# Two edits to an attention and Fourier-mixing kernel: where the transposed outputs of attention are kept, and how the very last product leaves PSUM

## The chip, the cores and the metric

The kernel runs on one core of one Trainium2 chip. The metric is the device time of one execution in microseconds (us). Three executions of the kernel before took 1701.39, 1704.11 and 1705.67 us, so their median is 1704.11 us.

## The reference, cut to what matters

Two independent blocks over 2048 tokens of width 1024 are computed and stood side by side in the output's columns.

```python
# A: causal attention in a window of 256, 32 heads of 32
qkv = x @ wqkv                                   # 2048 x 1024 @ 1024 x 3072
scores = q @ k.T * 32 ** -0.5                    # kept where 0 <= query - key < 256
a = softmax(scores) @ v                          # then the heads side by side
a = a @ wo                                       # 1024 x 1024
# B: real part of a two-dimensional Fourier transform by matrices
y = dft_seq_re @ (x @ dft_hid_re.T) - dft_seq_im @ (x @ dft_hid_im.T)
out = concatenate([a, y], axis=-1)               # 2048 x 2048
```

All of it is in float32. The kernel holds each operand as a pair of float16 tiles, a high part and a low part, and multiplies three of the four pairings (`PASSES`, line 48).

## The kernel before, in words

**The stages.** First come the products for q, k and v (lines 939 to 975). Then the products of B run, in units that a list orders (lines 758 to 761, 1143 to 1191). Last comes the product with `wo` in eight turns of two row tiles each (lines 1196 to 1206). All the large products but the first ones go through `seven` (line 1037): seven products of half the size in place of eight, written to three PSUM banks called a, b and c in the order a, b, a, c, a, b, a. A bank is 512 float32 columns of 128 partitions. Every product is twelve matmuls of 512 columns, four blocks of depth by three passes.

**Attention is woven into this.** `attention` (line 211) is a generator, and `tick` (line 373) takes steps from it between the matmuls of the large products, so that TensorE alternates between them. It works in blocks of 128 queries of two heads. Four blocks make a chunk of 512 queries; there are 64 chunks, 8 groups of heads by 2 pairs of heads by 4 chunks of the sequence. `mm` and `vec` keep the written order on TensorE and, at first, on VectorE; the rest is ordered by the scheduler of the tile layer. It gives each tile of a pool a buffer, and makes the first writer of a new tile wait for the last user of the buffer.

**What a chunk goes through at its end.** `v_step` (line 295) multiplies the weights of two blocks with v into a PSUM bank `pv`, and VectorE sums its pieces into the chunk's tile `o` (line 323, the "reduce" below; two per chunk). After the second reduce `o_step` (line 327) normalises `o` in place (VectorE line 332, GpSimd line 334), makes the pair of high and low parts in a tile `ohl` (ScalarE line 337, GpSimd line 338), and issues a transposing DMA from `ohl` into a tile `ot` (line 340). Three blocks later another DMA stores `ot` to a scratch tensor `ots` in DRAM (line 360), from where the last stage loads it (line 1008). Both DMAs are issued by SP, as are the transposes of the weights of each block (line 277) and nearly all loads.

**The buffers of these three.** `o`, `ohl` and `ot` are taken from one ring of three buffers, `tag="o", bufs=3` (lines 301, 336 and 339). Which of the three buffers a tile gets is settled when the program is built, by which comes free first. In the built program 10 of the 64 first reduces wait for DMA queues and 54 for GpSimd; most of the transposes of line 340 wait for the store of the chunk before, which holds the buffer that they write.

**The last product.** In the last of the eight turns the product at position 6 goes on adding to bank a, as two halves of 256 columns (lines 1048 to 1066). After both halves VectorE evicts one (line 1062) and ScalarE the other (line 1064); each is then stored by a DMA of its own from SP. Nothing is left for TensorE then.

Of the kernel before, what the change touches and what calls it, by code (L numbers as in the profile page):

```python
# [9 lines left out]
F32 = mybir.dt.float32  # L10
F32R = mybir.dt.float32r
F16 = mybir.dt.float16
# [3 lines left out]
AF = mybir.ActivationFunctionType  # L16
ALU = mybir.AluOpType
AX = mybir.AxisListType

P = 128  # L20
# [3 lines left out]
DH = 32  # L24
# [29 lines left out]
def fused_kernel(ctx: ExitStack, tc: tile.TileContext, xa, wqk, wv, wo, xb, wd, cs, out):  # L54
# [58 lines left out]
    def mm(*args, **kwargs):  # L113
        with tc.issue_after(fixed[0].ins) if fixed else nullcontext():
            fixed[:] = [nc.tensor.matmul(*args, **kwargs)]  # L115
        return fixed[0]
# [94 lines left out]
    def attention():  # L211
# [83 lines left out]
        def v_step(b):  # L295

            g, hp, sc, i = blocks[b]
            pvb = ps_v.tile([P, CH], F32, tag="pv", name=f"pv_{b}")
            pvt = pvb[:, :4 * VW].rearrange("p (r h w) -> p r h w", r=2, h=2)
            if (g, hp, sc) not in cur:  # L300
                cur[g, hp, sc] = att.tile([P, QB, 2, DH + 1], F32, tag="o", bufs=3, name=f"o_{g}_{hp}_{sc}")
            for r in (1, 0):
                qb = sc * QB + i + r
                nb = min(qb + 1, 3)
                nt = min(nb, 2)
                d = st[b + r]

                def weights(part, j, kb):
                    if nb == 3 and kb == 0:
                        return d["z"][:, part * 2 + j]  # L310
                    return d["t"][:, (part * 2 + j) * nt + kb - (nb - nt)]

                seq = [(0, kb) for kb in range(nb)] + [(1, kb) for kb in range(nb)]
                for j in range(2):
                    at = j * VW
                    for m, (part, kb) in enumerate(seq):
                        w = VW if part == 0 else DH + 1
                        k = qb + 1 - nb + kb
                        mm(pvt[:, r, j, :w], weights(part, j, kb),
                           vts[g, hp, k // QB][:, k % QB, at:at + w],  # L320
                                         start=(m == 0), stop=(m == len(seq) - 1),
                                         skip_group_check=True)
            nc.vector.tensor_reduce(cur[g, hp, sc][:, i:i + 2], pvt.rearrange("p r h (k w) -> p r h w k", k=2),
                                    axis=AX.X, op=ALU.add)
            del st[b], st[b + 1]

        def o_step(g, hp, sc):

            o = cur.pop((g, hp, sc))
            rs = att.tile([P, 2 * QB], F32, tag="rs", name=f"rs_{g}_{hp}_{sc}")  # L330
            on = o.rearrange("p i h w -> p (i h) w")
            nc.vector.reciprocal(rs, on[:, :, DH])
            on = on[:, :, :DH]
            nc.gpsimd.tensor_tensor(on, on, rs.unsqueeze(2).to_broadcast([P, 2 * QB, DH]), op=ALU.mult)
            o = o[:, :, :, :DH]
            ohl = att.tile([P, QB, 2, DH, 2], F16, tag="o", bufs=3, name=f"ohl_{g}_{hp}_{sc}")
            nc.scalar.activation(ohl[:, :, :, :, 0], o, AF.Copy)
            nc.gpsimd.tensor_tensor(ohl[:, :, :, :, 1], o, ohl[:, :, :, :, 0], op=ALU.subtract)
            ot = att.tile([P, QB, P], F16, tag="o", bufs=3, name=f"ot_{g}_{hp}_{sc}")
            nc.sync.dma_start_transpose(ot, ohl.rearrange("p i h d a -> p (i h d a)"))  # L340
            store_o.append((ots[sc, g, hp].rearrange("c a t -> (c a) t"), ot.rearrange("p i q -> p (i q)")))

# [691 lines left out]
        part = lambda u, k: (lambda h, d: u[:, h, HG * k + d])  # L1034
        oq[q] = (whole(t1, 0), part(u1, 0), part(u2, 1), whole(t1, 1), part(u2, 0), whole(t2, 1), part(u1, 1))

    def seven(name, q, lhs, rhs, y1, y2, f, out_y, hook, where=None, parts=1):

        where = where or {r: (ps_m, perm[(k - turns[0]) % 3]) for k, r in enumerate("abc")}
        turns[0] += 1  # L1040

        banks = {r: pool.tile([P, CH], F32, tag=f"m{t}", name=f"{name}_{r}") for r, (pool, t) in where.items()}
        copy = lambda y, ps: behind_act.__setitem__(slice(None), [nc.scalar.activation(y, ps, AF.Copy, scale=f)])
        add = lambda y, ps: behind.__setitem__(
            slice(None), [nc.vector.scalar_tensor_tensor(y, ps, f, y, op0=ALU.mult, op1=ALU.add)])  # L1045
        for pos in range(7):
            ps = banks["abacaba"[pos]]
            if pos == 6 and parts > 1:
                out_y(2 * q, y1[:, :1], 0)
                w = CH // parts  # L1050
                for e in range(parts):
                    cols = slice(e * w, e * w + w)
                    m = 0
                    for k in range(4):
                        for hl, hr in PASSES:
                            mm(ps[:, cols], lhs[pos](hl, k), rhs(pos)[:, hr, k, cols], start=False,
                               stop=(m == 11), skip_group_check=True)
                            m += 1
                for e in range(parts):
                    cols = slice(e * w, e * w + w)  # L1060
                    if e % 2 == 0:
                        nc.vector.tensor_scalar(y1[:, 1, cols], ps[:, cols], f, None, op0=ALU.mult)
                    else:
                        nc.scalar.activation(y1[:, 1, cols], ps[:, cols], AF.Copy, scale=f)
                    out_y(2 * q, y1[:, 1:, cols], CH + e * w)
                return
            m = 0
            for k in range(4):
                for hl, hr in PASSES:
                    mm(ps, lhs[pos](hl, k), rhs(pos)[:, hr, k], start=(m == 0 and pos < 2),  # L1070
                                     stop=(m == 11), skip_group_check=True)
                    m += 1
                    if m % 4 == 0:
                        tick(4)
            if pos == 0:

                nc.scalar.activation(banks["c"], ps, AF.Copy)
            elif pos == 1:
                copy(y2[:, 1], ps)
            elif pos == 2:  # L1080
                copy(y2[:, 0], ps)
            elif pos == 3:
                copy(y1[:, 0], ps)
            elif pos == 4:
                add(y2[:, 1], ps)
            elif pos == 5:
                add(y2[:, 0], ps)
                out_y(2 * q + 1, y2)
            else:
                copy(y1[:, 1], ps)  # L1090
                out_y(2 * q, y1)
            hook(pos)
# [4 lines left out]
    with tc.tile_pool(name="pb", bufs=1) as pb:  # L1097
# [4 lines left out]
        def ytile():  # L1102
            ny[0] += 1
            return ybufs[ny[0] % 4]
# [91 lines left out]
        for q in range(NT // 2):  # L1196
# [6 lines left out]
                                                        y.rearrange("p e c -> p (e c)")),  # L1203
                  lambda turn: None,
                  {r: (ps_o, k) if q % 2 and k < 2 else (ps_m, perm[k]) for k, r in enumerate("abc")},
                  2 if q == NT // 2 - 1 else 1)


def _layout(inputs):
# [45 lines left out]
```

## Time and profile before

| | |
|---|---|
| median of three executions | 1704.11 us |
| the profiled execution's own time | 1701.5 us |
| its span, first to last instruction | 1699.8 us |
| TensorE busy | 1688.6 us, 99% of the span |
| VectorE, ScalarE, GpSimd busy | 1299.0, 1168.5, 575.2 us |
| granted TensorE clock over the span | 1.000 |
| chunks: reduces of line 323, transposes of line 340, stores of line 360 | 128, 64, 64 |

TensorE is busy nearly all the time, so time can be won or lost only where it waits, and before its first and after its last matmul. A row of the view of waits names the engine and the line that waited, what it waited for, the sum in us, how often, and the longest. A row of the timeline gives start, duration, engine, line, operation, tiles and shape, and in brackets the idle time of the engine before it with what ended it. PE is TensorE, DVE VectorE, ACT ScalarE, POOL GpSimd, SPq the queue of SP.

### The profile page before, as it was taken

Reading aid. Unit: us, or ns where it says so; the run is one execution under the profiler, and the core shown is the slowest. Engines: PE = TensorE matmul, PEld = TensorE weight load, DVE = VectorE, ACT = ScalarE, POOL = GpSimd, SP = SyncE. Lnnn points to the kernel's source line nnn. Section 1 sums busy time; section 2 is a strip of 40 time slices with the busy share of each in tenths; the row PEclk is TensorE's granted clock in tenths of the full one; section 3 lists DMA queues with packets and bytes.
Section 4 is the critical chain, followed back from the end, with each engine's and each line's share of the span. In section 5 each row is a group of like instructions: output and inputs, shape, how many; then the busy total and the mean of one; then the engine's idle time right before and its main releaser. Section 6 shows DMA issues by size and latency. Waiting matters only on the chain.

```text
span 1699.8 us, 30887 instructions
## 1 busy us (share of the span) xinstructions
PE 1688.6 (99%) x11007; PEld 847.7 (50%) x11007; DVE 1299.0 (76%) x2223; ACT 1168.5 (69%) x2035; POOL 575.2 (34%) x874
## 2 busy tenths in 40 slices
PE   9999999999999999999999999999999999999999
PEld 4444544555555555555554555545545545444444
DVE  7657787888987789897688896688876698687442
ACT  4476666676876787887787886688877688563322
POOL 0001222344434441444423565434555425411000
PEclk9999999999999999999999999999999999999999
DMA  6677999999999985987997999986989976866431
GB/s 244 240 267 245 252 289 269 282 264 306 256 240 209 211 220 127 206 194 184 232 251 236 199 186 176 227 197 127 190 161 204 226 183 137 177 180 121 115 99 75
DMA packets 469899, 348.63 MB, mean 205 GB/s; under 512 B 376944, under 2 KB 409968, under 8 KB 468848
## 3 DMA queue, kind: packets, MB, share of 16 engines
q1 hardware_dynamic: 462064, 321.48, 75.7%
q0 software_dynamic: 7680, 25.17, 9.5%
q8 instruction: 86, 1.41, 0.4%
q14 instruction: 69, 0.57, 0.1%
HBM read 166.99 MB, written 106.17 MB: 161 GB/s over the span
## 4 chain that ended last, share of the span: by engine, by line
PE 90%; DVE 3%; DMA 3%; ACT 2%; issue 1%; SPq 0%; POOL 0%; DVEq 0%; ACTq 0%; POOLq 0%
PE p_a L115 25%; PE pv L115 13%; PE p_b L115 12%; PE pq L115 10%; PE pk L115 10%; PE p_c L115 6%; PE po_a L115 5%; PE s L115 3%; PE po_b L115 2%; PE far L115 1%; PE po_c L115 1%; DMA ots<-ot 1%; DMA raw_wo<-in_wo_dram 1%; DVE reg L850 0%; DMA t<-hl 0%
## 5 line engine op out<-in xcount | busy, mean ns | idle before, releaser
L271 ACT ACTIVATE s<-s,bias,escs 128x256 f32<-128x256 f32 (+1 forms) x512 | 270.0, 528 | 11.7
L289 POOL TENSOR_SCALAR_AFFINE_SELECT z<-t 128x512 f16<-128x512 f16 x224 | 183.8, 828 | 162.2 <-PE pv L115 140.3
L264 ACT ACTIVATE bias<-mx,pshift,escs 128x2 f32<-128x2 f32 x256 | 98.4, 384 | 172.0 <-DVE mx L261 171.3
L275 DVE TENSOR_TENSOR hl<-s,hl 128x512 f16<-128x512 f32 (+1 forms) x256 | 170.2, 665 | 51.6 <-ACT hl L274 50.8
L115 PEld LDWEIGHTS <-reg 128*128 128x128 f16 x1344 | 128.9, 98 | 141.5
L291 POOL TENSOR_SCALAR_AFFINE_SELECT t<-t 128x512 f16<-128x512 f16 x224 | 187.8, 847 | 11.3
L115 PE MATMUL p_a<-reg,un_c 128*128 128x512 f16 x768 | 181.4, 379 | 0.6 <-DVE reg L850 0.3
L115 PE MATMUL pk<-reg,wu_k 128*128 128x512 f16 x768 | 174.2, 379 | 0.0
L268 POOL TENSOR_SCALAR mark<-bias 128x1 f32<-128x1 f32 x128 | 52.5, 410 | 358.3 <-ACT bias L264 333.6
L261 DVE TENSOR_REDUCE mx<-s 128x2 f32<-128x512 f32 (+1 forms) x256 | 170.9, 668 | 3.5
L115 PE MATMUL pv<-reg,reg 128*128 128x512 f16 x768 | 172.5, 379 | 0.0
L115 PEld LDWEIGHTS <-un_c 128*128 128x128 f16 x1152 | 109.9, 97 | 121.5 <-issue 2.2
L115 PEld LDWEIGHTS <-un_b 128*128 128x128 f16 x1152 | 109.6, 97 | 117.7 <-issue 0.9
L115 PEld LDWEIGHTS <-un_a 128*128 128x128 f16 x1152 | 109.4, 97 | 116.5
L115 PE MATMUL pq<-reg,wu_q 128*128 128x512 f16 x696 | 156.3, 379 | 0.0
L274 ACT ACTIVATE hl<-s 128x512 f16<-128x512 f32 (+1 forms) x256 | 148.8, 581 | 6.9 <-DMA t<-hl 1.4
L115 PE MATMUL p_a<-reg,un_b 128*128 128x512 f16 x576 | 136.4, 379 | 0.3 <-DVE y L1045 0.2
L115 PE MATMUL p_c<-reg,un_a 128*128 128x512 f16 x576 | 136.5, 379 | 0.0
L115 PE MATMUL p_b<-reg,un_b 128*128 128x512 f16 x576 | 136.3, 379 | 0.1
L115 PE MATMUL p_a<-reg,un_a 128*128 128x512 f16 x576 | 136.1, 379 | 0.0
L259 DVE COPY_PREDICATED s<-upper,far 128x256 f32<-128x256 uint32 x224 | 94.3, 421 | 46.3 <-PE s L115 45.3
L115 PEld LDWEIGHTS <-qk 96*128 96x128 f16 x1056 | 87.7, 97 | 66.4 <-issue 4.9
(216 smaller groups left out, 3139.7 us busy)
## 6 DMA issues: line engine op xcount, KB each, us to landing
raw_u<-in_cs_dram SPq DMA_DIRECT2D x64, 512.0 KB, 5.0
qk<-qk SPq DMA_DIRECT2D x64, 384.0 KB, 4.7
out_dram<-y POOLq DMA_DIRECT2D x72, 256.0 KB, 6.3
raw_wd<-in_wd_dram SPq DMA_DIRECT2D x24, 512.0 KB, 5.6
vs<-yv SPq DMA_DIRECT2D x32, 264.0 KB, 4.5
vt<-vs SPq DMA_DIRECT2D x64, 132.0 KB, 4.7
qk<-yq SPq DMA_DIRECT2D x32, 256.0 KB, 4.5
raw_wo<-in_wo_dram SPq DMA_DIRECT2D x16, 512.0 KB, 8.4
```

The lines of the kernel that those rows point to most:

```text
L115: fixed[:] = [nc.tensor.matmul(*args, **kwargs)]
L259: nc.vector.copy_predicated(s[:, :, P:], upper2, d["far"] if nb == 3 else never2)
L261: nc.vector.tensor_reduce(mx, sv, axis=AX.X, op=ALU.max, negate=True)
L264: nc.scalar.activation(bias, mx, AF.Identity, bias=pshift, scale=es)
L268: marks[:] = [nc.gpsimd.tensor_scalar(mark, bias[:, 0:1], 1.0, None, op0=ALU.mult)]
L271: nc.scalar.activation(sv[:, h], sv[:, h], AF.Exp, bias=bias[:, h:h + 1], scale=es)
L274: nc.scalar.activation(hi, sv, AF.Copy)
L275: behind[:] = [nc.vector.tensor_tensor(lo, sv, hi, op=ALU.subtract)]
L289: nc.gpsimd.affine_select(out=z, in_=pk, compare_op=ALU.is_gt, fill=0.0, base=0, pattern=[[0, 4], [-1, P]], channel_multiplier=1)
L291: nc.gpsimd.affine_select(out=pk, in_=pk, compare_op=ALU.is_ge, fill=0.0, base=0, pattern=[[0, 4], [1, P]], channel_multiplier=-1)
```

## The change

The first edit is in attention. `o` becomes a flat tile in a ring of two buffers, and `ohl` gets a tile of its own with one buffer. There is no tile for `ot` any more: the transposing DMA writes into the first bytes of the chunk's own `o`, read as float16, whose sums have been used up by then. The second edit is in the last turn of the last stage. Position 6 writes to two PSUM banks of its own, 384 columns and then 128 columns, and starts them fresh. What bank a held before (the sum of positions 0, 2 and 4) is evicted by ScalarE after position 4. VectorE then makes each of the two results as a scaled bank plus that evicted sum, into tiles of `ytile`, the 384 columns while the 128 are being multiplied. Each is stored from SP as before.

```diff
-                cur[g, hp, sc] = att.tile([P, QB, 2, DH + 1], F32, tag="o", bufs=3, name=f"o_{g}_{hp}_{sc}")
+                cur[g, hp, sc] = att.tile([P, QB * 2 * (DH + 1)], F32, tag="o", bufs=2, name=f"o_{g}_{hp}_{sc}")
...
-            ohl = att.tile([P, QB, 2, DH, 2], F16, tag="o", bufs=3, name=f"ohl_{g}_{hp}_{sc}")
+            ohl = att.tile([P, QB, 2, DH, 2], F16, tag="ohl", bufs=1, name=f"ohl_{g}_{hp}_{sc}")
...
-            ot = att.tile([P, QB, P], F16, tag="o", bufs=3, name=f"ot_{g}_{hp}_{sc}")
+            ot = held_o.bitcast(F16)[:, :QB * P].rearrange("p (i q) -> p i q", i=QB)
             nc.sync.dma_start_transpose(ot, ohl.rearrange("p i h d a -> p (i h d a)"))
...
+        ends = [(pool_, at_, w) for pool_, at_, w in (parts or ())]
+        halves = [pool_.tile([P, CH], F32, tag=f"m{t_}", name=f"{name}_e{k}") for k, ((pool_, t_), _, _) in enumerate(ends)]
+        lasts = [ytile()[:, 0, :w] for _, _, w in ends]
...
-                            mm(ps[:, cols], lhs[pos](hl, k), rhs(pos)[:, hr, k, cols], start=False,
+                            mm(e[:, :w], lhs[pos](hl, k), rhs(pos)[:, hr, k, cols], start=(m == 0),
...
-                    if e % 2 == 0:
-                        nc.vector.tensor_scalar(y1[:, 1, cols], ps[:, cols], f, None, op0=ALU.mult)
-                    else:
-                        nc.scalar.activation(y1[:, 1, cols], ps[:, cols], AF.Copy, scale=f)
-                    out_y(2 * q, y1[:, 1:, cols], CH + e * w)
-                return
+                    nc.vector.scalar_tensor_tensor(o, e[:, :w], f, y1[:, 1, cols], op0=ALU.mult, op1=ALU.add)
+                    out_y(2 * q, o.unsqueeze(1), CH + at_)
+                continue
...
             elif pos == 4:
                 add(y2[:, 1], ps)
+                if ends:
+                    copy(y1[:, 1], ps)
...
-                  2 if q == NT // 2 - 1 else 1)
+                  (((ps_o, 2), 0, 3 * P), ((ps_o, 3), 3 * P, P)) if q == NT // 2 - 1 else None)
```

Up to the last product the instructions of every engine stand in the same order as before; what changes there is what some of them wait for. On SP this is the piece around the transpose of chunk `6_0_2` (group 6, first pair, third chunk; 1211.2 us in the profiled execution) into `ot`, with the counters that each row waits for. The DMAs from SP use eight completion counters in turn, DMAHW0 to DMAHW7; each waits for the one that had its counter before, and the store two rows above the transpose uses DMAHW0.

```order
L277 DMA_TRANSPOSE t_207_15226<-hl_207_15223 128x8x128 [waits DMAHW7_49,DVE_49]
L360 DMA ots_59<-ot_6_0_1_15051 128x512 [waits DMAHW0_49]
L277 DMA_TRANSPOSE t_208_15273<-hl_208_15270 128x4x128 [waits DVE_49,DMAHW1_49,PE_49,Pool_49]
L340 DMA_TRANSPOSE ot_6_0_2_15315<-ohl_6_0_2_15312 128x4x128 [waits DMAHW2_49,DMAHW0_49,Pool_49]
L232 DMA vt_6_1_1_15506<-vs_58 128x4x132 [waits DMAHW3_49,PE_49]
L277 DMA_TRANSPOSE t_209_15353<-hl_209_15350 128x8x128 [waits DMAHW4_49,DVE_49]
```

The same piece of the changed kernel, whose line numbers are two higher:

```order
L277 DMA_TRANSPOSE t_207_15176<-hl_207_15173 128x8x128 [waits DMAHW7_49,DVE_49]
L362 DMA ots_59<-o_6_0_1_14849 128x512 [waits DMAHW0_49]
L277 DMA_TRANSPOSE t_208_15223<-hl_208_15220 128x4x128 [waits DVE_49,DMAHW1_49,PE_49,Pool_49]
L342 DMA_TRANSPOSE o_6_0_2_15111<-ohl_6_0_2_15262 128x4x128 [waits DMAHW2_49,Pool_49]
L232 DMA vt_6_1_1_15455<-vs_58 128x4x132 [waits DMAHW3_49,PE_49]
L277 DMA_TRANSPOSE t_209_15302<-hl_209_15299 128x8x128 [waits DMAHW4_49,DVE_49]
```

The transpose no longer waits for DMAHW0, the store of the chunk before; it still waits for GpSimd, which makes `ohl`, and for the eighth DMA before it.

On VectorE, at the first reduce of chunk `6_1_0`, two chunks later (the 105th of the 128 reduces, at 1237.38 us in the profiled execution), before:

```order
L259 COPY_PREDICATED s_214_15651<-upper_90,far_1040 128x2x128 [waits PE_49]
L261 TENSOR_REDUCE mx_214_15657<-s_214_15651 128x2 [waits DVE_49]
L122 SCALAR_TENSOR_TENSOR un33_a_15677<-raw_u33_0_15324,sc_u33_15635,un33_a_15677 128x1024 [waits DMAHW5_49,Activation_49]
L323 TENSOR_REDUCE o_6_1_0_15688<-pv_208_15687 128x132 [waits DMAHW3_49,DMAHW2_49,DMAHW6_49,DMAHW0_49,PE_49]
L807 TENSOR_TENSOR raw_u33_0_15324<-raw_u33_0_15324,raw_u33_1_15129 128x512 [waits DVE_49]
L275 TENSOR_TENSOR hl_213_15612<-s_213_15598,hl_213_15612 128x512 [waits DMAHW5_49,Activation_49]
```

And now:

```order
L259 COPY_PREDICATED s_214_15599<-upper_90,far_1040 128x2x128 [waits PE_49]
L261 TENSOR_REDUCE mx_214_15605<-s_214_15599 128x2 [waits DVE_49]
L122 SCALAR_TENSOR_TENSOR un33_a_15625<-raw_u33_0_15273,sc_u33_15583,un33_a_15625 128x1024 [waits DMAHW5_49,Activation_49]
L324 TENSOR_REDUCE o_6_1_0_15636<-pv_208_15635 128x132 [waits DMAHW2_49,DMAHW3_49,PE_49,Pool_49]
L809 TENSOR_TENSOR raw_u33_0_15273<-raw_u33_0_15273,raw_u33_1_15079 128x512 [waits DVE_49]
L275 TENSOR_TENSOR hl_213_15560<-s_213_15546,hl_213_15560 128x512 [waits DMAHW5_49,Activation_49]
```

DMAHW2 is the transpose of chunk `6_0_2` and DMAHW3 its store, so this reduce waits for the same store in both kernels. In the changed kernel 62 of the 64 first reduces wait for such a store, that of the chunk two before; in the kernel before 10 wait for DMA queues.

At the end of VectorE's program, before:

```order
L1045 SCALAR_TENSOR_TENSOR yo6_1_20171<-po6_a_20172,fo_110,yo6_1_20171 128x512 [waits DMAHW7_49,PE_49,Activation_49]
L1045 SCALAR_TENSOR_TENSOR yo6_1_20171<-po6_b_20173,fo_110,yo6_1_20171 128x512 [waits PE_49,Activation_49]
L1045 SCALAR_TENSOR_TENSOR yo7_1_20269<-po7_a_20270,fo_110,yo7_1_20269 128x512 [waits PE_49,Activation_49]
L1045 SCALAR_TENSOR_TENSOR yo7_1_20269<-po7_b_20271,fo_110,yo7_1_20269 128x512 [waits PE_49,Activation_49]
L1062 TENSOR_SCALAR yo7_0_20268<-po7_a_20270,fo_110 128x256 [waits PE_49]
```

And now:

```order
L1047 SCALAR_TENSOR_TENSOR yo6_1_20107<-po6_b_20109,fo_110,yo6_1_20107 128x512 [waits PE_49,Activation_49]
L1047 SCALAR_TENSOR_TENSOR yo7_1_20205<-po7_a_20206,fo_110,yo7_1_20205 128x512 [waits PE_49,Activation_49]
L1047 SCALAR_TENSOR_TENSOR yo7_1_20205<-po7_b_20207,fo_110,yo7_1_20205 128x512 [waits PE_49,Activation_49]
L1063 SCALAR_TENSOR_TENSOR y1_6757<-po7_e0_20209,fo_110,yo7_0_20204 128x384 [waits DMASW2_49,DMASW3_49,PE_49,Activation_49]
L1063 SCALAR_TENSOR_TENSOR y2_6758<-po7_e1_20210,fo_110,yo7_0_20204 128x128 [waits DMASW1_49,DMASW0_49,PE_49]
```

The eviction of line 1062 is replaced by two additions, of 384 and of 128 columns, and ScalarE's last instruction is no longer the second half but the 512 columns of bank a after position 4.

More of the change, by code (lines that the diff above doesn't have):

```diff
@@ L322, in v_step @@
                                          skip_group_check=True)
-            nc.vector.tensor_reduce(cur[g, hp, sc][:, i:i + 2], pvt.rearrange("p r h (k w) -> p r h w k", k=2),
+            o = cur[g, hp, sc].rearrange("p (i h w) -> p i h w", i=QB, h=2)
+            nc.vector.tensor_reduce(o[:, i:i + 2], pvt.rearrange("p r h (k w) -> p r h w k", k=2),
                                     axis=AX.X, op=ALU.add)
@@ L327, in o_step @@
         def o_step(g, hp, sc):
-            o = cur.pop((g, hp, sc))
+            held_o = cur.pop((g, hp, sc))
+            o = held_o.rearrange("p (i h w) -> p i h w", i=QB, h=2)
             rs = att.tile([P, 2 * QB], F32, tag="rs", name=f"rs_{g}_{hp}_{sc}")
@@ L1035, in o_blocks, with seven @@
         oq[q] = (whole(t1, 0), part(u1, 0), part(u2, 1), whole(t1, 1), part(u2, 0), whole(t2, 1), part(u1, 1))
-    def seven(name, q, lhs, rhs, y1, y2, f, out_y, hook, where=None, parts=1):
+    def seven(name, q, lhs, rhs, y1, y2, f, out_y, hook, where=None, parts=None):
         where = where or {r: (ps_m, perm[(k - turns[0]) % 3]) for k, r in enumerate("abc")}
@@ L1045, in seven @@
             slice(None), [nc.vector.scalar_tensor_tensor(y, ps, f, y, op0=ALU.mult, op1=ALU.add)])
+        ends = [(pool_, at_, w) for pool_, at_, w in (parts or ())]
+        halves = [pool_.tile([P, CH], F32, tag=f"m{t_}", name=f"{name}_e{k}") for k, ((pool_, t_), _, _) in enumerate(ends)]
+        lasts = [ytile()[:, 0, :w] for _, _, w in ends]
         for pos in range(7):
             ps = banks["abacaba"[pos]]
-            if pos == 6 and parts > 1:
+            if ends and pos == 6:
                 out_y(2 * q, y1[:, :1], 0)
-                w = CH // parts
-                for e in range(parts):
-                    cols = slice(e * w, e * w + w)
+                for e, o, (_, at_, w) in zip(halves, lasts, ends):
+                    cols = slice(at_, at_ + w)
                     m = 0
@@ L1055, in seven @@
                         for hl, hr in PASSES:
-                            mm(ps[:, cols], lhs[pos](hl, k), rhs(pos)[:, hr, k, cols], start=False,
+                            mm(e[:, :w], lhs[pos](hl, k), rhs(pos)[:, hr, k, cols], start=(m == 0),
                                stop=(m == 11), skip_group_check=True)
                             m += 1
-                for e in range(parts):
-                    cols = slice(e * w, e * w + w)
-                    if e % 2 == 0:
-                        nc.vector.tensor_scalar(y1[:, 1, cols], ps[:, cols], f, None, op0=ALU.mult)
-                    else:
-                        nc.scalar.activation(y1[:, 1, cols], ps[:, cols], AF.Copy, scale=f)
-                    out_y(2 * q, y1[:, 1:, cols], CH + e * w)
-                return
+                    nc.vector.scalar_tensor_tensor(o, e[:, :w], f, y1[:, 1, cols], op0=ALU.mult, op1=ALU.add)
+                    out_y(2 * q, o.unsqueeze(1), CH + at_)
+                continue
             m = 0
```

## The prediction

> **What bounds the kernel now.** I began with the page's busy times and then asked for the waits of TensorE alone (engine, tile and line, what was waited for, us in total, how often, the longest).
>
> ```profile
> PE 1688.6 (99%) x11007; PEld 847.7 (50%) x11007; DVE 1299.0 (76%) x2223; ACT 1168.5 (69%) x2035; POOL 575.2 (34%) x874
> ```
>
> ```profile
> PE far L115 <- DVE s L259: 4.3, 2, 3.2
> PE wps L735 <- DVE reg L727: 1.2, 1, 1.2
> PE p_a L115 <- DVE y L1045: 0.5, 2, 0.3
> PE pq L115 <- DMA wx<-in_xa_dram: 0.3, 1, 0.3
> PE p_a L115 <- DVE reg L850: 0.3, 1, 0.3
> PE p_a L115 <- ACT p_c L1077: 0.2, 1, 0.2
> ```
>
> TensorE bounds it. Of the span of 1699.8 us all but 11.2 are TensorE's own work, which the change leaves as it is except for the last product. The waits add up to 6.8 us, 1.2 of them before the first matmul. Most of what is left lies after the last one. So two places matter: the one long wait, 3.2 us, and the end. The end, in the timeline:
>
> ```profile
> 1687.89 2.75 PE L115 MATMUL po_a<-wx,uo 128*128 128x512 f16 x12
> 1688.09 0.69 ACT L1043 ACTIVATE yo<-po_c,fo 128x512 f32<-128x512 f32 x1 [1.90 <-PE po_c L115]
> 1688.80 8.44 SPq L1202 DMA_DIRECT2D out_dram<-yo  x4
> ...
> 1690.48 2.75 PE L115 MATMUL po_b<-wx,raw_o 128*128 128x512 f16 x12
> 1690.75 0.75 DVE L1045 SCALAR_TENSOR_TENSOR yo<-po_a,fo,yo 128x512 f32<-128x512 f32 x1 [14.79 <-PE po_a L115]
> ...
> 1693.07 2.78 PE L115 MATMUL po_a<-wx,uo 128*128 128x256 f16 x24
> ...
> 1695.89 0.48 DVE L1062 TENSOR_SCALAR yo<-po_a,fo 128x256 f32<-128x256 f32 x1 [1.80 <-PE po_a L115]
> 1696.41 0.47 ACT L1064 ACTIVATE yo<-po_a,fo 128x256 f32<-128x256 f32 x1 [7.63 <-DVE yo L1062]
> ```
>
> The last matmul ends at 1695.85, and then the two evictions run one after the other: both read bank a, and ScalarE's idle time is ended by VectorE's eviction. They end at 1696.88, the issue of the last store at 1697.24, and the span at 1699.8.
>
> **The last product, the certain part.** It removes 24 matmuls of 256 columns and adds twelve of 384 and twelve of 128. From start to start, twelve matmuls of 512 columns take 2.59 us (1687.89 to 1690.48), 216 ns each; 24 of 256 take about 2.62, 109 each. That is 0.42 ns a column and 2 ns besides, so one of 384 columns takes 162 ns, twelve 1.95. Matmuls of 128 columns stand elsewhere in the trace:
>
> ```profile
> 1240.01 0.22 PE L115 MATMUL far<-qk,qk 96*128 96x128 f16 x1 [3.21 <-DVE s L259]
> 1240.06 0.22 PE L115 MATMUL s<-qk,qk 96*128 96x128 f16 x1
> 1240.12 0.22 PE L115 MATMUL s<-qk 96*128 96x128 f16 x1
> ```
>
> They start 50 to 60 ns apart; with 55, twelve take 0.66, and the two parts 2.61: TensorE ends where it ended, within 0.05 us.
>
> The Trainium skill ("TensorE: Matmul & The Clock Gate", section "Back-to-back issue gap") speaks against narrow matmuls: it gives about 81 ns as the sustained spacing of pairs of weight load and matmul at 128 columns. By it the twelve would take 0.97 us, and the gain below would be about 0.34 instead of 0.65. The rows above, each with a weight load of its own, show 55, so I take 55.
>
> What follows the matmuls: VectorE's addition over 512 columns takes 0.75 us and its eviction of 256 took 0.48, about 1.05 ns a column and 0.21 fixed, so 0.62 for 384 and 0.35 for 128 (estimates from these two rows; the 128 lies in any case between 0.2 and 0.48). The 384 columns are complete at about 1693.07 + 1.95 + 0.16 = 1695.18, where the 0.16 is what a matmul lasts beyond its spacing (the last of 256 runs to 1695.85, 0.27 after its start). Their addition runs from 1695.22 to 1695.84, beside the narrow matmuls. The 128 columns are complete at 1695.84, and their addition runs from 1695.88 to 1696.23, where ScalarE ended at 1696.88 before. That is 0.65 earlier. SP ended the issue of the last store 0.36 us after its eviction; by that it is done with the first of the two at 1696.20, just as the second is wanted, and a loss of 0.05 is possible there. The store behind it and the end cost what they cost before. Bounds: from the two ends for the narrow addition, 0.5 to 0.8 us gained. Hidden is the new eviction of bank a after position 4. It is ScalarE's (0.69 by the row at 1688.09), it can start after VectorE's 0.75 at 1690.75, that is by 1691.5, and ends by 1692.2, 3 us before its first use. ScalarE has nothing else to do there (7.63 us idle), and no later matmul writes to bank a.
>
> **The buffers of attention.** No instruction is added or moved here; waits change. Removed is the wait of SP's transposes for the store of the chunk before. What SP waited for, and two neighbours from the list of all waits:
>
> ```profile
> SPq L340 <- DMA ots<-ot: 42.0, 26, 5.7
> ```
>
> ```profile
> POOL z L289 <- DMA t<-hl: 20.9, 10, 4.2
> ACT ohl L337 <- POOL o L334: 30.6, 32, 3.9
> DVE o L323 <- DMA ots<-ot: 5.7, 1, 5.7
> ```
>
> SP's 42.0 us hold up everything queued behind on SP: the transposes of block weights, loads of v, q and k. But TensorE's list names no wait for a DMA in attention; late transposes reached GpSimd alone, an engine that is busy for 34% of the span, and the matmuls use its result six blocks after the scores (`LAG`, line 39). So freeing SP is worth nothing directly. It can gain no more than TensorE's waits in attention, and it can cost something only by bringing loads and stores together, which is the second rival. `ohl` in a single buffer waits for the previous chunk's transpose to land; in the row above ScalarE waited only for GpSimd there, so that costs nothing.
>
> Added is a wait of VectorE: the first reduce of a chunk waits for the store of the chunk two before. Ten of the 64 first reduces waited for DMA queues before, 62 do now. One of the ten is the last row above, and it makes TensorE's long wait:
>
> ```profile
> 1222.08 2.07 SPq L768 DMA_DIRECT2D raw_u<-in_cs_dram  x2
> 1227.53 0.57 SPq L360 DMA_DIRECT2D ots<-ot  x1
> 1230.79 0.49 PE L115 MATMUL pv<-vt,t 128*128 128x66 f16 x12
> 1237.38 0.43 DVE L323 TENSOR_REDUCE o<-pv 128x132 f32<-128x264 f32 x1 [5.70 <-DMA ots<-ot]
> 1239.53 0.42 DVE L259 COPY_PREDICATED s<-upper,far 128x256 f32<-128x256 uint32 x1
> ```
>
> The store is issued at 1227.53, behind two loads of `raw_u`, and lands 9.6 us later; the reduce could have run at 1231.7. Queued behind it on VectorE are subtractions for the next unit and the masking of line 259, for which `far` on TensorE waits: 5.70 us of VectorE's wait became 3.21 of TensorE's, so 2.5 were slack. In the changed kernel this very reduce waits for the very same store, since the chunk two before holds its buffer. SP's rows ahead of that store stand in the same order, and this is the longest that SP itself waited for from 1217 to 1228:
>
> ```profile
> SPq L232 <- PE pv L115: 3.6, 1, 3.6
> ```
>
> The removed wait is not in that list. SP stood waiting for TensorE before it issued the loads, so that whatever it gains earlier is lost again there, and the burst forms as it did. So I keep the 3.2 us where they are.
>
> Do the other 52 new waits bite? The stores and how long they take to land, and the distance from a store's issue to the reduce that would wait for it, first and last of 62 (3.5 us the shortest, 28 the longest, 7.6 the median; the last row is the landing of the last pair's store alone):
>
> ```profile
> L360 SPq DMA_DIRECT2D ots<-ot x64: 319/570/2020, 202.8 to 1476.9; - x64
> ...
> DMA to landing us min/median/max: 1.9/3.6/9.6
> ```
>
> ```profile
> 220.68 0.42 DVE L323 TENSOR_REDUCE o<-pv 128x132 f32<-128x264 f32 x1
> ```
>
> ```profile
> 1458.97 0.57 SPq L360 DMA_DIRECT2D ots<-ot  x1
> ```
>
> ```profile
> 1462.50 0.43 DVE L323 TENSOR_REDUCE o<-pv 128x132 f32<-128x264 f32 x1
> ```
>
> ```profile
> DMA to landing us min/median/max: 6.3/6.3/6.3
> ```
>
> Pair by pair, the landing came after the reduce's start in two cases only: the one above, and the last, which lands 6.3 us after issue, 2.8 after the reduce. There no scores are left to mask, and 2.8 is hardly above the slack of 2.5; I cost it at nothing. Drawing landings and distances at random instead gives 3 or 4 waits an execution, 4.3 us for VectorE, but only 0.5 beyond the slack. So the new waits cost 0 to 0.5 here, and 3.2 for each store that meets a burst of loads as the one at 1227.53 did.
>
> **The sum.** 1701.5 (the profiled execution, span 1699.8 and 1.7 around it) - 0.65 = 1700.85. The three runs have their median at 1704.11, 2.6 above the profiled execution, for a reason that this trace cannot show; the 0.65 comes off that as well: 1703.5.
>
> **The rivals.** First, the long wait goes: transposes issued up to 5.7 us earlier spread SP's traffic, so that the store near 1227.53 lands in time. For it speaks the 42.0 us; against it the 3.6 us for which SP stood waiting for TensorE ahead of that burst. It takes 3.2 more off, 1700.3. If the 2.6 us of the typical run were of this kind too, 1697.7.
>
> Second, slower: VectorE's new waits. The mechanism is the one above, at chunks whose store is issued behind loads of the next unit. One more such wait gives 1703.5 + 3.2 = 1706.7, two 1709.9. It decides as soon as a store lands more than 2.5 us after its reduce could run. For it speaks that half the distances are below 7.6 us while landings reach 9.6; against it that of 62 pairs none but the known one did it.
>
> Third, the narrow matmuls wait for their weight loads. The page has the length of one:
>
> ```profile
> L115 PEld LDWEIGHTS <-un_a 128*128 128x128 f16 x1152 | 109.4, 97 | 116.5
> ```
>
> At 97 ns each, one behind the other, twelve narrow matmuls take 1.16 us in place of 0.66, the gain falls to 0.15, and the time is 1704.0. Against it stand the rows with 55 ns. The section of the Trainium skill cited above, with its 81 ns, is a weaker form of this.
>
> Fourth, the change does not do what it says at the end: the addition of 384 columns waits for the last matmul after all, and the two run one after the other, 0.62 + 0.35 = 0.97 us where 0.99 stood (1695.89 to 1696.88): 1704.1.
>
> **How the numbers follow.** Chances: forecast 0.55, first rival 0.20, second 0.14, third 0.07, fourth 0.04. About 0.3%, 5.1 us, is what a measurement of this kernel can tell from no change. The forecast, the third and the fourth lie inside it. Of the first rival 0.07 goes beyond (the typical run's 2.6 us gone too); of the second 0.06 (two waits or more). That makes faster 0.07, same 0.87, slower 0.06. The range goes from the first rival, 1700.3, less 0.8 for a part of TensorE's other short waits, 1699.5, to one added wait, 1706.7; the three runs' own spread (2.7 below the median, 1.6 above) lies inside it around 1703.5.
>
> **What would show it.** Right: the last addition of 128 columns ends 0.35 to 0.45 us after the last matmul, and the span's end comes 0.65 nearer to it; the waits of SP's transposes for stores are gone from SP's list; TensorE's list still has one wait of about 3 us for line 259's masking near 1240, and VectorE's first reduces wait for stores a few times, 5 to 12 us in all. Wrong: VectorE's waits for stores above 15 us with several waits of TensorE behind them (slower), or no wait of TensorE over 1.5 us in attention (first rival), or a wait of TensorE for something that is not in the list above.

## The result and the profile after

| | before | after |
|---|---|---|
| median, us (runs) | 1703.76 (6) | 1716.38 (6) |
| range, us | 1701.24 to 1707.13 | 1711.61 to 1717.82 |
| profiled execution, us | 1701.5 | 1711.61 |
| its span, us | 1699.8 | 1709.9 |

The changed kernel is slower: ratio 1.0068, 95% interval 1.0053 to 1.0083, or 12.6 us between the medians. The forecast was 1703.5. The profiled execution of after is the fastest of its six, so its trace holds 10.1 of the 12.6 us. Its page, busy times first:

```profile
PE 1691.2 (99%) x11007; PEld 847.6 (50%) x11007; DVE 1298.1 (76%) x2224; ACT 1170.4 (68%) x2035; POOL 575.7 (34%) x874
```

The same number of matmuls kept TensorE busy for 2.6 us longer. What it waited for, the two longest rows from the list of TensorE's waits (us in total, times, longest):

```profile
PE far L115 <- DVE s L259: 7.8, 2, 6.5
PE pv L115 <- DVE sc_u L122: 4.3, 1, 4.3
```

The wait for line 259's masking grew from 4.3 to 7.8 us, and one of 4.3 us is new. That adds up: 3.5 + 4.3 + 2.6 of longer matmuls - 0.65 gained at the end = 9.75 of the 10.1 us. Most of the rest is a wait for a load at the start, 0.8 us where it was 0.3. In the list of all waits, the rows that answer to those quoted of before:

```profile
POOL z L289 <- DMA t<-hl: 26.1, 9, 9.4
...
DVE o L324 <- DMA ots<-o: 14.0, 2, 8.8
...
ACT hl L274 <- DMA t<-hl: 10.5, 5, 4.9
```

The 42.0 us that SP's transposes stood behind stores are gone, as they should be. VectorE's reduces wait for stores 14.0 us instead of 5.7, in two chunks. The shorter wait, 5.16 us near 1478, is that of the last pair of chunks, and TensorE waits for nothing there. The longer one is the very reduce that waited before, for the very same store. The timeline around it:

```profile
1233.85 0.57 SPq L362 DMA_DIRECT2D ots<-o  x1
1233.89 1.75 POOL L1137 DMA_DIRECT2D out_dram<-y  x2
...
1234.53 5.29 SPq L277 DMA_TRANSPOSE t<-hl  x1
...
1242.17 1.03 PE L115 MATMUL p_c<-reg,un_a 128*128 128x512 f16 x4
1246.89 0.43 DVE L324 TENSOR_REDUCE o<-pv 128x132 f32<-128x264 f32 x1 [8.81 <-DMA ots<-o]
...
1249.19 0.42 DVE L259 COPY_PREDICATED s<-upper,far 128x256 f32<-128x256 uint32 x1
1249.66 0.26 PE L115 MATMUL far<-qk,qk 96*128 96x128 f16 x1 [6.47 <-DVE s L259]
...
1250.26 2.34 PE L115 MATMUL p_c<-reg,un_a 128*128 128x512 f16 x5
```

The reduce could run at 1238.08, 4.2 us after the store's issue, exactly as before; only the store now lands after 12.9 us and not 9.6. It is the slowest of the 64; their median has not moved from 3.6:

```profile
DMA to landing us min/median/max: 2.0/3.6/12.9
```

VectorE's 8.81 us become 6.47 of TensorE's, a slack of 2.3, as the prediction had it (2.5). What comes on top is in the last row: five matmuls of 512 columns take 2.34 us where four had taken 1.03. The view of busy times by window (PE busy is the second figure, PEclk the third from the end):

```profile
1240.00:1250.00 10.00, 3.53 (x19) 1.70 (x18) 3.08 (x6) 1.34 (x3) 1.81 (x3) 0.85 0.81 96
1250.00:1254.00 4.00, 4.00 (x15) 1.64 (x13) 3.97 (x8) 3.56 (x7) 2.94 (x4) 0.53 0.76 108
...
962.00:968.00 6.00, 4.04 (x36) 2.27 (x36) 5.41 (x12) 4.81 (x9) 4.34 (x7) 0.72 0.83 169
```

The granted clock is 0.53 over the 4 us after the stall. In before TensorE stood for 3.21 us at this place, until 1240.01, and its clock did not fall afterwards:

```profile
1240.00:1250.00 10.00, 9.77 (x73) 5.08 (x73) 9.10 (x17) 8.52 (x15) 5.46 (x8) 1.00 0.76 148
```

The Trainium skill ("TensorE: Matmul & The Clock Gate", section "Part 1: The HAM clock gate (the "warmup" mystery)") says that the clock goes to half when TensorE is idle for a window of about 3.4 us. These two traces agree: 3.21 us cost their own length, 6.47 and 4.32 cost up to 2 us more each. Two runs below do not: with the second edit alone the same wait was 2.83 us, and the clock was 0.60 and 0.55 in the two stretches of 2 us behind it; with the first edit alone a wait of 2.21 us near 962 was followed by 0.72 and 0.50. The runs decide: a wait shorter than 3.4 us can bring the clock down too, and no length is shown here below which it is safe.

The new wait, which ends at 963.96, is no store's doing. Two transposes of block weights are issued at 936.47 and 943.96, with the accumulating output transfers of GpSimd (line 1137) beside them:

```profile
936.47 1.56 SPq L277 DMA_TRANSPOSE t<-hl  x1
938.08 1.77 POOL L1137 DMA_DIRECT2D out_dram<-y  x2
938.13 1.42 SPq L342 DMA_TRANSPOSE o<-ohl  x1
```

How long the two took to land, and what the transfers moved from 942 to 950 us:

```profile
DMA to landing us min/median/max: 13.6/13.8/13.9
```

```profile
DMA packets 1205, 0.62 MB, mean 77 GB/s; under 512 B 1124, under 2 KB 1124, under 8 KB 1204
```

In before the same rows, issued within 0.4 us of the same times, read:

```profile
DMA to landing us min/median/max: 6.3/6.8/7.4
```

```profile
DMA packets 2944, 1.48 MB, mean 185 GB/s; under 512 B 2749, under 2 KB 2749, under 8 KB 2943
```

So the DMA engines, about as busy there (a share of 1.24, and 1.26 in before), moved under half in that stretch, transposed weights came 7 us later, and the delay passed from ScalarE and GpSimd over VectorE to TensorE. If the 2.6 us of longer matmuls are split evenly over the two places, this one costs about 5.6 us and the late store about 4.6 more than in before (estimates from these rows). In this execution, then, the late store is under half of the loss.

The end came as forecast. Its timeline:

```profile
1702.30 0.69 ACT L1045 ACTIVATE yo<-po_a,fo 128x512 f32<-128x512 f32 x1 [2.76 <-DVE yo L1047]
...
1703.83 2.78 PE L115 MATMUL po_e<-wx,uo 128*128 128x384 f16 x24
...
1706.04 0.96 DVE L1063 SCALAR_TENSOR_TENSOR y<-po_e,fo,yo 128x384 f32<-128x384 f32 x2 [1.19 <-PE po_e L115]
1706.68 0.81 SPq L1203 DMA_DIRECT2D out_dram<-y  x2
```

From the first matmul of the last product to the end of the span it was 6.70 us (1693.07 to 1699.77) and is 6.05 (1703.83 to 1709.88).

### The profile page after: what moved, and what is told of

Read it like the earlier page. It is cut to its first block, busy times and chain, and to the rows that moved or that the text cites. A ratio compares the mean times of both kernels' runs of the same rounds, so it can differ in the third digit from the quotient of the medians.

```text
span 1709.9 us, 31012 instructions
## 1 busy us (share of the span) xinstructions
PE 1691.2 (99%) x11007; PEld 847.6 (50%) x11007; DVE 1298.1 (76%) x2224; ACT 1170.4 (68%) x2035; POOL 575.7 (34%) x874
## 3 DMA queue, kind: packets, MB, share of 16 engines
q0 software_dynamic: 7680, 25.17, 9.5%
## 4 chain that ended last, share of the span: by engine, by line
PE 85%; DMA 5%; DVE 4%; ACT 3%; issue 2%; SPq 0%; POOL 0%; DVEq 0%; ACTq 0%; POOLq 0%
PE p_a L115 23%; PE pv L115 13%; PE p_b L115 11%; PE pq L115 10%; PE pk L115 9%; PE p_c L115 6%; PE po_a L115 5%; PE s L115 3%; PE po_b L115 2%; DMA ots<-o 2%; PE far L115 1%; PE po_c L115 1%; DMA t<-hl 1%; DMA raw_u<-in_cs_dram 1%; DVE hl L275 1%
## 5 line engine op out<-in xcount | busy, mean ns | idle before, releaser
L291 POOL TENSOR_SCALAR_AFFINE_SELECT t<-t 128x512 f16<-128x512 f16 x224 | 187.0, 844 | 11.3
L274 ACT ACTIVATE hl<-s 128x512 f16<-128x512 f32 (+1 forms) x256 | 148.8, 581 | 15.9 <-DMA t<-hl 10.5
```

Source lines behind the costliest of these rows:

```text
L274: nc.scalar.activation(hi, sv, AF.Copy)
L291: nc.gpsimd.affine_select(out=pk, in_=pk, compare_op=ALU.is_ge, fill=0.0, base=0, pattern=[[0, 4], [1, P]], channel_multiplier=-1)
```

## The experiments

Theory 1: VectorE's new waits for stores that land late make the loss (the second rival). Theory 2: SP, freed of its waits, issues transfers into each other, and transposed weights come late. Runs of one group were taken together with the kernel before; in the first four below it had 1702.18 us (27 executions).

**The second edit alone**: before, with only the split of the last product.

```diff
-                  2 if q == NT // 2 - 1 else 1)
+                  (((ps_o, 2), 0, 3 * P), ((ps_o, 3), 3 * P, P)) if q == NT // 2 - 1 else None)
```

> The kernel before with the second edit alone: the last product in banks of 384 and 128 columns, attention's ring as before. All theories expect 0.65 us off, which the two traces show at the end (from the first matmul of the last product to the end of the span 6.70 us before, 6.05 after): 1703.1 for 1703.8. If it is slower by 5 us or more, the end has a cost that the trace of after hides, and the theories on the buffers of attention fall.

Measured 1701.68 us, ratio 1.0002 (0.9993 to 1.0012). A gain of the 0.65 us seen in the timeline would be 0.04% and lies within that interval; this edit does no harm that can be measured.

**The first edit alone**: before, with only the buffers of attention changed.

```diff
-                cur[g, hp, sc] = att.tile([P, QB, 2, DH + 1], F32, tag="o", bufs=3, ...)
+                cur[g, hp, sc] = att.tile([P, QB * 2 * (DH + 1)], F32, tag="o", bufs=2, ...)
...
-            ot = att.tile([P, QB, P], F16, tag="o", bufs=3, ...)
+            ot = held_o.bitcast(F16)[:, :QB * P].rearrange("p (i q) -> p i q", i=QB)
```

> The kernel before with the first edit alone: the buffers of o, ohl and ot as in the changed kernel, the last product as before. All theories on the buffers expect the whole loss, 12.6 + 0.65 = 13 us: about 1717 for 1703.8, and in the trace one or more waits of TensorE of 4 us and more in attention.

Measured 1712.14 us, ratio 1.0064 (1.0041 to 1.0087). That is less than the 1717 expected, but within the interval the whole loss is in this edit. In its trace TensorE waits 5.1 us for line 259 and 2.2 us behind late transposes; VectorE waits 14.8 us for stores.

**A third buffer of sums**: the changed kernel, in which a reduce now waits for the store of the chunk three before. The room comes from four small tiles.

```diff
-cur[...] = att.tile([P, QB * 2 * (DH + 1)], F32, tag="o", bufs=2, ...)
+cur[...] = att.tile([P, QB * 2 * (DH + 1)], F32, tag="o", bufs=3, ...)
-mx: bufs=6, bias: bufs=6, mark: bufs=2
+mx: bufs=2, bias: bufs=4, mark: bufs=1, rs: bufs=1
```

> The changed kernel with three buffers for o in place of two (room made by fewer buffers for four tiny tiles). The first reduce of a chunk then waits for the store of the chunk three before, some 17 us earlier, while SP's transposes stay free of stores. Theory 1, VectorE's waits for late stores stall TensorE: the loss goes, 1703 or below, no wait of VectorE for a store. Theory 2, SP that no longer waits for stores crowds its DMAs, which then land late and hold up ScalarE and VectorE through the buffers of the block weights: the loss stays or nearly, 1712 to 1718, with transposes that take 12 us and more to land. Half and half would be 1709.

Measured 1703.0 us, ratio 1.0007 (0.9991 to 1.0023). The order of instructions is that of the changed kernel and SP is as free, yet most of the loss is gone: 0.8 us by the medians, where it was 12.6. No reduce waits for a store any more. The late transposes stay, though: its profiled execution (1707.55 us) has TensorE waiting at 964 us as after does:

```profile
POOL z L289 <- DMA t<-hl: 36.6, 10, 9.5
...
PE pv L115 <- DVE sc_u L122: 3.5, 1, 3.5
```

**One buffer for each**: before, with sums, halves and transposed outputs in a tag and a buffer each.

```diff
-o, ohl, ot: tag="o", bufs=3
+o: tag="o", bufs=1; ohl: tag="ohl", bufs=1; ot: tag="ot", bufs=1
```

> The kernel before with one buffer each for o, ohl and ot in place of the common ring: the first reduce waits for GpSimd alone, and every transpose of line 340 waits for the store of the chunk before. Theory 1 (VectorE's waits for stores): no such wait is left, so at or below the kernel before, 1700 to 1704. Theory 2 (crowding by a freed SP): SP waits as much as before or more, so no crowding, 1700 to 1704 too. If it is slow like the changed kernel, both fall, and what is left is where the tiles lie.

Measured 1705.8 us, or 1705.1 without one execution of 2277.51, which the ratio leaves out too: 1.0014 (1.0002 to 1.0026). That is above the 1700 to 1704 that both theories gave. SP waits for stores (59.4 us), VectorE does not; the loss is 2 us by the ratio, 3 by the medians. Late transposes at 936 us (11.6 to 13.8 us to land) and TensorE's waits behind them are here too. So they are not peculiar to an SP that has been freed, which speaks against Theory 2 as I had put it.

**The small tiles alone**, the control of the run with three buffers (in the group of this run, the next, the later store and the two buffers below, the kernel before had 1703.19 us, 16 executions): two buffers of sums again, the cuts as there.

```diff
-mx: bufs=6, bias: bufs=6, mark: bufs=2
+mx: bufs=2, bias: bufs=4, mark: bufs=1, rs: bufs=1
```

> Control for the run with three buffers of sums: the changed kernel with two buffers of sums as it was, and only the cuts that had made room (mn 6 to 2, bias 6 to 4, mark 2 to 1, rs to 1). Under both theories the cuts alone are worth nothing: 1714 to 1719 us. If it comes out at 1703, the cuts and not the third buffer took the loss away, and the reading of that run falls.

Measured 1720.41 us, ratio 1.0093 (1.0057 to 1.0129), a little above the 1714 to 1719 expected. The cuts by themselves do not help, so the third buffer is what took the loss away. The profiled execution of the control, 1723.04 us, shows the second store of the changed kernel at its worst, that of the last pair of chunks:

```profile
1469.96 1.67 POOL L1137 DMA_DIRECT2D out_dram<-y  x2
1471.10 0.57 SPq L362 DMA_DIRECT2D ots<-o  x1
1471.74 2.25 POOL L1137 DMA_DIRECT2D out_dram<-y  x2
...
1486.98 0.43 DVE L324 TENSOR_REDUCE o<-pv 128x132 f32<-128x264 f32 x1 [12.53 <-DMA ots<-o]
...
1487.47 0.21 PE L115 MATMUL pv<-vt,z 128*128 128x66 f16 x1 [6.32 <-DVE o L324]
```

No masking is needed for TensorE to stand here: the reduce that waits holds the bank `pv`, which the next matmuls need.

**The store one block earlier**: the changed kernel, with each store a block (4 to 5 us) earlier in SP's order.

```diff
-                if j == 1 and store_o and (b >= nblk or blocks[b][3] == 3):
+                if j == 1 and store_o and (b >= nblk or blocks[b][3] == 2):
```

> The changed kernel with each store put into SP's order one block of the attention earlier (4 to 5 us, at the third block of a chunk and not the fourth); same tiles, same buffers, same waits. In the profile of the changed kernel the store is issued 2.1 to 34.8 us (median 10.5) behind the landing of its transpose, so nearly all can go earlier; the two stores that were late for their reduce by 8.7 and 5.0 us would be late by 4.3 and 0.6. Theory 1 (VectorE's waits for late stores make the loss): about 1704 to 1708 us, under half of the loss is left, VectorE's waits on stores under 6 us in total. Theory 2 (SP without its waits issues its transfers into each other, and transposed weights come late): the transfers are as crowded as before, 1714 to 1718 us, with the late transposes at 936 to 960 us still there.

Measured 1706.17 us, ratio 1.0019 (0.9998 to 1.0039), from 1699.69 to 1717.63. No reduce waits for a store, and about three quarters of the loss is gone. Its profiled execution is the slowest of the seven, 1717.63 us, and there late transposes alone stop TensorE, for 5 us each:

```profile
PE pv L115 <- POOL z L289: 5.6, 1, 5.6
PE p_a L115 <- ACT y L1045: 4.9, 1, 4.9
PE pv L115 <- DVE sc_u L122: 4.0, 1, 4.0
```

**Two blocks earlier** (`blocks[b][3] == 1`; in its group, with the two runs of plain transfers below, the kernel before had 1702.25 us, 24 executions):

> The changed kernel with the stores two blocks earlier in SP's order (second block of a chunk; one block earlier gave 1706.2, one later 1758.3). Theory 1: no reduce waits for a store, 1702 to 1707 us, as with one block or a little better. Theory 2: the rest of the loss is the crowding, which stays or grows, since SP may now wait for a transpose to land ahead of the store (2 to 13 us after its issue) with the next transposes queued behind it: 1707 to 1716 us, the late transposes of weights at 936 to 960 us still in the profile.

Measured 1706.15 us, ratio 1.0018 (0.9997 to 1.0038), from 1700.91 to 1714.58: the same as one block. That is inside what Theory 1 gave (1702 to 1707) and just below Theory 2 (1707 to 1716). No reduce waits for a store. The two transposes of 936 and 944 us, which Theory 2 had late here too, land in 3.7 and 5.6 us. The profiled execution has one long wait left, 5.2 us for line 289 at 1474, behind a transpose that took 16.9 us.

**One block later**, behind the next chunk's transpose:

```diff
-                if j == 1 and store_o and (b >= nblk or blocks[b][3] == 3):
+                if j == 1 and (store_o if b >= nblk else len(store_o) > 1 and blocks[b][3] == 0):
```

> The changed kernel with each store put into SP's order one block later (the first block of the next chunk, behind the next chunk's transpose). In the profile of the changed kernel the reduce comes 0.2 to 25.5 us behind the landing of its store, below 2.7 us at one chunk in four; 4.5 us later some 34 of 62 reduces would wait. Theory 1: VectorE waits some 60 to 120 us in total for stores and a good part reaches TensorE, 1735 to 1790 us. Theory 2: the stores' place in the order matters little, 1712 to 1722 us.

Measured 1758.27 us, ratio 1.0331 (1.0314 to 1.0347). VectorE's row in the list of all waits:

```profile
DVE o L324 <- DMA ots<-o: 81.5, 27, 10.9
```

With 81.5 us of such waits the kernel is 55 us slower than before. With no block, one block earlier and one later we have 1716, 1706 and 1758: the distance from store to reduce moves the time the way that Theory 1 says.

**Two buffers for transposed outputs**: before with one `o`, one `ohl`, two `ot` and the cuts; SP no longer waits for the store just behind, and no reduce waits for a store.

```diff
-o, ohl, ot: tag="o", bufs=3
+o: tag="o", bufs=1; ohl: tag="ohl", bufs=1; ot: tag="ot", bufs=2
```

> The kernel before with one buffer of sums, one of halves and two of transposed outputs, each with a tag of its own (room by the same cuts). SP no longer waits for the store just behind, as in the changed kernel, and VectorE's reduce waits for the lo half of the chunk before and never for a store. Theory 1: 1701 to 1706 us, as the run with one buffer of each. Theory 2: SP is as free as in the changed kernel and so 1711 to 1717 us.

Measured 1703.15 us, ratio 1.0006 (0.9995 to 1.0017), the time of before. This does not show that a freed SP costs nothing, though. In before a late store stops TensorE for 3.21 us near 1240; no reduce can wait for one here, nor with the third buffer, with one buffer for each, or with the store earlier, and still none of these five runs beats before. From their medians and the 3.21 us, with the 0.65 us gained at the end where that edit is in, the late transposes cost them some 3 to 8 us (an estimate; the 3.21 is of one execution). They stop TensorE in all five traces, whether SP waits or not.

So Theory 1 holds for the larger part of the difference between the kernels. The third buffer takes 11.8 of the 12.6 us away (12.6 less 0.8), but 3.2 of them are a wait that before pays as well; that leaves about 8.6 us for the changed kernel's waits for stores and 4 for the late transposes (estimates from medians). Why these come with every change of the buffers, Theory 1 does not say, and it leaves the cause of the late landings open. The three pile-ups at which TensorE came to stand, near 940, 1240 and 1475 us, all have GpSimd's accumulating transfers in them, which are issued from 917.5 to 1563.3 us. The last pair writes them plainly, so that the first half's sums are left out of the output.

**Plain transfers, in the changed kernel:**

```diff
-                nc.gpsimd.dma_start(dst, src, accum_op=ALU.add)
+                nc.gpsimd.dma_start(dst, src)
```

> The changed kernel with GpSimd's 96 output transfers of the attention stage (917 to 1563 us, 256 KB each) written plainly, not accumulated onto what is in memory: the first half's sums are left out of the output. Instructions, order, sizes and waits stay. The three places where transfers pile up (936 to 960, 1233 to 1250, 1466 to 1487 us) all have two to four of these transfers in flight beside transposes. If the accumulating transfers are what the stores of the transposed outputs stand behind, these land in under 8 us, no reduce waits more than 1.5 us for one, and the time falls by 10 to 16 us against the changed kernel, to 1698 to 1706 us. If the burst of loads that SP issues is the cause, as the prediction held, the late landings and 1712 to 1718 us stay.

Measured 1697.83 us, ratio to before 0.9975 (0.9964 to 0.9987), just below the 1698 to 1706 expected. One reduce still waits for a store, for 1.8 us where 1.5 was the most expected:

```profile
DVE o L324 <- DMA ots<-o: 1.8, 1, 1.8
```

The slowest store, still the one near 1240 behind the loads, lands in 7.1 us and no longer in 12.9, half of them within 3.2 instead of 3.6; the two transposes of 936 and 944 us land in 4.7 and 6.4 instead of 13.6 and 13.9:

```profile
DMA to landing us min/median/max: 1.7/3.2/7.1
```

```profile
DMA to landing us min/median/max: 4.7/5.6/6.4
```

**Plain transfers, in the kernel before:** the same line.

> The same edit in the kernel before, as the pair of the run above: plain transfers, the first half's sums left out. If accumulating transfers cause the late landing, the one long wait near 1240 us (3.4 us with what follows it) goes as well and the kernel comes out at 1695 to 1701 us; the difference between this run and its pair is then under 4 us, where 13 stand between the two kernels themselves. If not, 1700 to 1704 us, and the difference stays about 13.

Measured 1697.4 us, ratio 0.9969 (0.9959 to 0.9980). Its slowest store lands in 7.1 us too, the one near 1240 in 6.7 instead of 9.6, and TensorE's long wait there is gone. The two ratios differ by 0.0006, with 0.0015 as the uncertainty of that difference (both half intervals squared and added): 1 us give or take 2.6. By the medians it is 0.4 us, where 12.6 lie between the kernels as they are. Without the accumulation the change costs nothing that can be measured. The loads ahead of that store stand as they did, so they are not enough to make its landing as late as it was; the prediction had named nothing but them.

## Why the prediction was wrong

- **TensorE bounds the kernel; only its waits and the end can move the time.** Right: 9.75 of 10.1 us are such waits, their effect on the clock, and the end.
- **The last product gains 0.65 us, and 55 ns is the spacing of narrow matmuls.** Right: 6.70 to 6.05 us. The 24 matmuls take 2.78 us as the 24 of 256 columns did, the two additions together 0.96 us as estimated (0.62 + 0.35), the added eviction is out of the way by 1702.99. The third and fourth rivals fall with it.
- **Freeing SP is worth nothing directly, and the halves' single buffer costs nothing.** The totals agree: ratios of 1.0007 and 1.0006 with SP free and no reduce behind a store. But these runs are spared the 3.2 us too, so something of that size, the late transposes, is hidden in them.
- **"The burst forms as it did. So I keep the 3.2 us where they are."** This is the step that failed first. Place, store and distance (4.2 us) were right, and so was the slack; the term mis-sized is the landing, 12.9 us for 9.6. It gave 6.47 us of TensorE's time for 3.21, and half speed behind it, which the sum did not have at all. I took the landing of one execution for fixed; the same store landed after 9.6, 9.2, 11.3 and 12.9 us in before, with each edit alone (second, then first) and in after, and after 2.0 us when it was issued a block earlier, ahead of the loads.
- **"The new waits cost 0 to 0.5 here."** Wrong by the runs, though not by the trace of after. Landings measured in the trace of before were set against the distances of before, pair by pair, and the one further pair found, the last, was costed "at nothing" because no scores are left to mask there. That pair's reduce waited 5.16 us in the profiled execution of after, and TensorE did not wait for it there. In the execution of the control it waited 12.53 us, and `pv` passed 6.32 of it on to TensorE. With the third buffer the waits for stores go, and 11.8 us with them.
- **"TensorE's list names no wait for a DMA in attention; late transposes reached GpSimd alone".** This is the second step that failed, a term put at nothing. The first half is true of before; the second is not quite, as ScalarE's line 274 waited 1.4 us for a transpose there. In after ScalarE waited 10.5 us for transposes, and a wait of TensorE of 4.32 us, with half speed behind it, stems from two of them that took 13.6 and 13.9 us. It was for something that is not in the list of before, one of the signs of being wrong that the prediction named. The five runs with no reduce behind a store came out 0 to 4 us above before by their medians, and up to 14 in a single execution (the one of 2277.51 left out).
- **The second rival, 0.14.** It had the larger part of the mechanism and the right place, and its condition (a landing over 2.5 us after the reduce could run) was met twice. Its price of 3.2 us a store was a poor guide: in the trace of after one store cost TensorE 6.47 us and half speed, the other nothing, and in the control's that other one 6.32. The late transposes are no part of it.
- **The first rival** went the other way: the long wait did not go, it doubled. Where it did go, in the five runs named above, the kernel was no faster.

Open: why the rate between 942 and 950 us falls to 77 to 113 GB/s in seven of the kernels with changed attention buffers, and not in before (185), with the second edit alone (184) or with the stores two blocks earlier (171) or one later (157), though the transfers of that place are issued within 0.4 us of the same times in before and after. Each of these rates is of one execution. Also open is what it is in the accumulating transfer that the others stand behind, since the plain form changes its handling by GpSimd as well (a median of 902 ns to issue one of `y`, then 552). No run that keeps the whole output beat the kernel before.

## What to carry to other kernels

When a compute engine is made to wait for a buffer until a store from it has landed, the distance from the store's issue to that wait must exceed the slowest landing under the worst traffic, not the median: here 4.2 us stood against a median of 3.6 and a maximum of 12.9. With a third buffer, or the store a block or two earlier, no reduce waited for a store in the profiled executions, and 1 to 4 us of the loss were left by the medians. A wait on a DMA queue, which holds only transfers back, was cheaper here than one on an engine that feeds TensorE: in before SP stood for 42.0 us and no wait of TensorE is seen behind it, while VectorE's waits for stores cost about 8.6 of the 12.6 us (the estimate above).

## What was not expected of the hardware

Accumulating output transfers, 96 of 256 KB, cost more than the bytes that the profile counts for them. The same 25.17 MB took 9.5% of the time of the DMA engines in before and after, and 5.4% and 5.5% when written plainly. Written plainly, they shorten the slowest store's landing from 12.9 to 7.1 us in the changed kernel and from 9.6 to 7.1 in before, and the kernel by 0.25 to 0.31%. With them, the DMA engines were reported about as busy in the stretch of 77 GB/s as in that of 185:

```profile
942.00:950.00 8.00, 8.00 (x42) 3.84 (x41) 7.14 (x15) 6.71 (x14) 2.81 (x4) 1.00 1.24 77
```

```profile
942.00:950.00 8.00, 8.00 (x47) 3.89 (x45) 7.68 (x15) 6.63 (x14) 4.31 (x6) 1.00 1.26 185
```

The first row is of after, the second of before; the last two columns are the DMA share and GB/s. Here the busy share of the DMA engines did not tell how much they moved.
